# Causal attention in one written-out order of steps, with mask and row minimum in one VectorE instruction, ahead of two feed-forward layers

## The chip, the cores and the metric

The kernel runs on one core of one Trainium2 chip. The metric is the device time of one execution in microseconds (us). A core has five engines that run beside each other, each through its own queue of instructions in order: TensorE (PE in the profile; its weight loads are listed as PEld), VectorE (DVE), ScalarE (ACT), GpSimd (POOL) and SyncE (SP, which here starts the transfers). Matmul results go to PSUM, of which the kernel makes eight banks of 128 x 512 fp32 numbers; everything else lies in SBUF.

## The reference

```python
scores = scale * np.matmul(q, k.transpose(0, 1, 3, 2))      # batch 2, heads 12, seq 448, head_dim 64
scores = np.where(np.triu(ones, k=1), -1e9, scores)
scores = scores - scores.max(-1, keepdims=True)
attn = np.exp(scores)
attn = attn / (attn.sum(-1, keepdims=True) + 1e-09)
x = np.matmul(attn, v)                                       # then (2*448, 12*64) = (896, 768)
h = x @ w_in                                                 # first layer, d_ff 2048
x = (h - np.tanh(h)) @ w_out
y = ((x @ w_a) * (x @ w_b)) @ moe2_w_out                     # second layer, d_ff 1536
```

The weights come in as 64-bit numbers, and the kernel turns them into fp32 itself.

## The kernel before

Attention goes by 12 pairs of heads (2 batches, 6 pairs each; the two heads of a pair are called e = 0 and 1). A pair has four chunks c of 112 query rows; chunk c needs only the first (c+1)*112 keys. So the work is 48 units j = (pair i, chunk c), and a loop over j issues, for every unit, steps of several units at once (a pipeline written by hand).

- `scores(j)` (L254 to L266): q and k of the pair are each split in a high and a low part in fp32r (`qkh`, `qkl`; by `split_qk`, on GpSimd at L248 and L251, for pair 0 on ScalarE at L250), and three products of 64-row operands are summed for each head in a bank of tag `s`. A fourth matmul for each head, of an identity and `mask` in bf16 (L266), adds the causal mask.
- `top(j)`: VectorE takes each head's row maximum from the bank (L271) and scales both by -scale (L272). `exps(j)`: ScalarE reads the bank and writes `p = exp(scale*s + m)` and the row sums (L283). The bank is free only after that.
- `turn_p(j-2)`: TensorE transposes the 112 x 112 blocks of p into banks of tag `t` (L298), which ScalarE (L309) or VectorE (L307) copies to `pt`.
- `values`: twice for each pair, v against `pt`, into the one bank of tag `o` (L319), half h = 0 (chunks 0 and 1) and half h = 1 (chunks 2 and 3).
- `weigh`, `turn_r`: reciprocal of the row sums (VectorE L328, L329), widened on GpSimd (L331), transposed (L337), copied to `y` (ScalarE L346); then x = o * y on VectorE (L349), its high part on ScalarE (L350), its low part on GpSimd (L351). L349 frees bank `o`.

Beside attention two other kinds of work are spread over the loop by the function `filler`. One is the weights' conversion, for each tile of 128 x 768 (or 640): two transfers (L116), a magnitude on ScalarE (L125), four bit operations on VectorE (L142, L144, L148, L152, one at the end of each unit from j = 16 on), a high part on ScalarE (L166) and a low part on GpSimd, after attention on VectorE (L168). The other is the first five hidden chunks of the first layer for batch 0 (`hidden`, 18 matmuls of 448 columns each at L194, all into the one bank of tag `h`): from j = 28 on up to five of these matmuls stand in each unit. When a group of 18 is done, tanh (ScalarE L429) and a subtraction (VectorE L426) must have read the bank before the next group may begin.

The banks are `s` 4, `o` 1, `t` 2, `h` 1. Attention stands in the order of the program text, on every engine. All that comes behind it (the rest of both layers, nearly all matmuls) is ordered by a scheduler at build time, which may also put such work between attention's last steps.

Of the kernel before, what the change touches and what calls it, by code (L numbers as in the profile page):

```python
# [28 lines left out]


# [18 lines left out]
def attention_moe_moe2(ctx, tc, q, k, v, w_in, w_out, w_a, w_b, w_o, out):  # L49
# [5 lines left out]
    XLAG = 7  # L55
    WEIGHTS_AT = 16
    GROUP_P = (2, 4, 3, 4)
# [23 lines left out]
    ident16 = const.tile([128, 128], BF16, name="ident16")  # L81
    mask = const.tile([128, 512], BF16, name="mask")
# [21 lines left out]
    at = {"load": 0, "abs": 0, "bits": 0, "step": 0, "halve": 0, "use": 0, "done": 0}  # L104
# [54 lines left out]
    def split():  # L159
        i = at["halve"]  # L160
        if i >= at["bits"] or i >= at["done"] + len(w_r.turns):
            return
        t = ts.pop(i)
        nk = t.shape[1]
        hi, lo = w_r.tile([([128, KD, 128], F32R, "wh"), ([128, KD, 128], F32R, "wl")])
        nc.scalar.copy(out=hi[:, 0:nk], in_=t.bitcast(F32))  # L166
# [4 lines left out]
        halves[i] = (hi, lo)  # L171
        at["halve"] += 1

# [29 lines left out]
    later_act, later_dve = [], []  # L203
# [3 lines left out]
    def attention(filler):  # L207
        with ExitStack() as st:
            inp = st.enter_context(tc.tile_pool(name="inp", bufs=3))
            pp = st.enter_context(tc.tile_pool(name="p", bufs=1))  # L210
            fixed = st.enter_context(tc.tile_pool(name="fixed", bufs=1))
            sp = st.enter_context(tc.tile_pool(name="small", bufs=4))
# [3 lines left out]
            pts = [fixed.tile([QC, 2, 2 * (h + 1), 2, QC], F32, name=f"pt{h}") for h in range(NQ // 2)]  # L216
            qk, qk2 = {}, {}
            sc, pr, sums, xf, ot = {}, {}, {}, {}, {}
            pairs = [(b, p) for b in range(B) for p in range(NPAIR)]
            units = [(i, c) for i in range(len(pairs)) for c in range(NQ)]  # L220
            def load(i, names):
                if i >= len(pairs):
                    return
                b, p = pairs[i]
                for nm in names:
                    if nm == "v":
                        for e in range(2):
                            nc.sync.dma_start(
                                out=vs[i % NV][:, :, e, :],
                                in_=v[b, 2 * p + e].rearrange("(c s) d -> s c d", s=QC),  # L230
                            )
                    else:
                        if nm == "q":
                            qk[i] = inp.tile([128, 2, S], F32, tag="qk", name="qk")
                        nc.sync.dma_start(
                            out=qk[i][:, int(nm == "k")], in_={"q": q, "k": k}[nm][b, 2 * p:2 * p + 2].rearrange("h d s -> (h d) s")
                        )

            def split_qk(i):

                if i >= len(pairs):
                    return
                hi = inp.tile([128, 2, S], F32R, tag="qkh", name="qkh", bufs=2)
                lo = inp.tile([128, 2, S], F32R, tag="qkl", name="qkl", bufs=2)
                t = qk.pop(i)
                for x in range(2):
                    if i:
                        nc.gpsimd.tensor_copy(out=hi[:, x], in_=t[:, x])  # L248
                    else:
                        nc.scalar.copy(out=hi[:, x], in_=t[:, x])  # L250
                    nc.gpsimd.tensor_tensor(out=lo[:, x], in0=t[:, x], in1=hi[:, x].bitcast(F32), op=ALU.subtract)  # L251
                qk2[i] = hi, lo

            def scores(j):  # L254

                i, c = units[j]
                n = (c + 1) * QC
                cs = slice(c * QC, n)
                sc[j] = [bank("s")[:QC, :n], bank("s")[:QC, :n]]
                hi, lo = qk2[i]  # L260
                for x, (a, b_) in enumerate(((hi, hi), (hi, lo), (lo, hi))):
                    for e in range(2):
                        r = slice(64 * e, 64 * e + 64)
                        nc.tensor.matmul(sc[j][e], a[r, 0, cs], b_[r, 1, :n], start=x == 0, stop=False)  # L264
# [3 lines left out]
            def top(j):  # L268
                m = sp.tile([QC, 2], F32, tag="m", name="m")
                for e, s in enumerate(sc[j]):  # L270
                    nc.vector.tensor_reduce(out=m[:, e:e + 1], in_=s, axis=mybir.AxisListType.X, op=ALU.max)  # L271
                nc.vector.tensor_scalar_mul(out=m, in0=m, scalar1=-scale)  # L272
                pr[j] = m

            def exps(j):
                i, c = units[j]
                n = (c + 1) * QC
                m = pr.pop(j)
                p = pp.tile([QC, 2, n], F32, tag=f"p{c}", name="p")
                if c == 0:  # L280
                    sums[i] = sp.tile([QC, NQ, 2], F32, tag="sum", name="sum", bufs=3)
# [5 lines left out]
                pr[j] = p  # L287

            def turn_p(j):

                i, c = units[j]
                p = pr.pop(j).rearrange("q h (k s) -> q (h k) s", s=QC)
                nb = 2 * (c + 1)
                for a in range(0, nb, GROUP_P[c]):
                    g = GROUP_P[c]
                    pst = bank("t")
                    for x in range(g):
                        nc.tensor.transpose(  # L298
                            out=pst[:QC, x * QC:(x + 1) * QC], in_=p[:, a + x], identity=ident[:QC, :QC]
                        )  # L300
                    out_ = pts[c // 2][:, :, :c + 1, c % 2]
                    if g == nb:
                        in_ = pst[:QC, :g * QC].rearrange("s (e k q) -> s e k q", e=2, q=QC)
                    else:
                        out_, in_ = out_[:, a // g], pst[:QC, :g * QC].rearrange("s (k q) -> s k q", q=QC)
                    if c == 0 or (c >= 2 and a):
                        later_dve.append(lambda o=out_, p=in_: nc.vector.tensor_copy(out=o, in_=p))  # L307
                    else:
                        later_act.append(lambda o=out_, p=in_: nc.scalar.copy(out=o, in_=p))  # L309

            def values(i, h):

                vt, o = vs[i % NV], bank("o") if h == 0 else ot[i]
                ot[i] = o
                for k_ in range(2 * h + 2):
                    c0 = max(2 * h, k_)
                    cs = slice(c0 * QC, (2 * h + 2) * QC)
                    for e in range(2):
                        nc.tensor.matmul(  # L319
                            o[64 * e:64 * e + 64, cs], vt[:, k_, e, :],  # L320
                            pts[h][:, e, k_, c0 - 2 * h:].rearrange("s c q -> s (c q)"),
                            start=k_ == 0, stop=k_ == 2 * h + 1, skip_group_check=True,
                        )

            def weigh(i):

                r = sums.pop(i)
                nc.vector.tensor_scalar_add(out=r, in0=r, scalar1=1e-9)  # L328
                nc.vector.reciprocal(out=r, in_=r)  # L329
                wide = sp.tile([QC, NQ, 2, D], F32, tag="wide", name="wide", bufs=2)  # L330
                nc.gpsimd.tensor_copy(out=wide, in_=r.unsqueeze(3).to_broadcast([QC, NQ, 2, D]))  # L331
                sums[i] = wide

            def turn_r(i):
                r, pst, o = sums.pop(i), bank("t"), ot.pop(i)
                for c in range(NQ):
# [3 lines left out]
                    )  # L340
                b, kk = pairs[i]
                if kk not in xh:
                    xh[kk], xl[kk] = [xp.tile([128, NT], F32R, tag=x, name=x) for x in ("xh", "xl")]
                hi, lo = [t[kk][:, b * S:(b + 1) * S] for t in (xh, xl)]
                x, y = [sp.tile([128, S], F32, tag=t, name=t, bufs=2) for t in "xy"]
                later_act.append(lambda: nc.scalar.copy(out=y, in_=pst[:, :S]))  # L346

                def divide():
                    nc.vector.tensor_tensor(out=x, in0=o[:, :S], in1=y, op=ALU.mult)  # L349
                    nc.scalar.copy(out=hi, in_=x)  # L350
                    nc.gpsimd.tensor_tensor(out=lo, in0=x, in1=hi.bitcast(F32), op=ALU.subtract)  # L351
# [266 lines left out]
```

## Time and profile before

| | us |
|---|---|
| median of 3 runs | 642.12 |
| the runs | 639.67, 642.12, 643.72 |
| span of the profiled execution | 639.7 |
| TensorE busy | 619.0 (97%) |
| VectorE busy | 419.3 (66%) |
| ScalarE busy | 268.2 (42%) |
| GpSimd busy | 82.1 (13%) |

The span of the profiled execution is also its own time; it is as long as the fastest of the three runs, 2.4 us below their median. Busy time counts an instruction from its start to its end, and neighbours on an engine overlap at their ends, so the pitch from one start to the next is somewhat shorter than the duration. [...]

### The profile page before, as it was taken

What the parts mean: (1) busy time and instruction counts of PE and PEld (TensorE: products, weight loads), DVE (VectorE), ACT (ScalarE), POOL (GpSimd) and SP (SyncE); (2) the same over time, 40 slices, a digit from 0 to 9 for tenths busy, and PEclk for the clock granted to TensorE, in tenths of its full rate; (3) what the DMA queues carried; (4) which work ended last, traced back from release to release, by engine and by line L of the source; (5) the groups of instructions that cost most, each with busy time, mean ns of one, the idle gap of its engine ahead of it and who ended that gap; (6) DMA issues with size and microseconds to landing.
All of it is one profiled execution on the core that took longest, in us unless ns stands there. A gap on an engine that the chain in (4) does not pass through costs nothing.

```text
span 639.7 us, 9131 instructions
## 1 busy us (share of the span) xinstructions
PE 619.0 (97%) x3496; PEld 538.7 (84%) x3496; DVE 419.3 (66%) x722; ACT 268.2 (42%) x545; POOL 82.1 (13%) x85
## 2 busy tenths in 40 slices
PE   8999888889999999999999999999999999999997
PEld 4766665567899988998889889999999989999997
DVE  4778655655488899977788986666730489862211
ACT  4777545545265555422544433334421444432000
POOL 4567844422100000000000000000000000000000
PEclk9997778989999999999999999999999999999999
DMA  6443332211144534543333244433230064500111
GB/s 182 120 129 95 94 93 86 56 42 42 42 140 150 189 107 148 172 140 119 112 100 99 99 149 125 123 99 99 99 99 1 2 196 148 162 38 1 50 63 61
DMA packets 64972, 65.08 MB, mean 102 GB/s; under 512 B 13984, under 2 KB 61856, under 8 KB 64928
## 3 DMA queue, kind: packets, MB, share of 16 engines
q1 hardware_dynamic: 64928, 64.50, 32.0%
q8 instruction: 27, 0.44, 0.3%
q14 instruction: 17, 0.14, 0.1%
HBM read 61.73 MB, written 2.75 MB: 101 GB/s over the span
## 4 chain that ended last, share of the span: by engine, by line
PE 92%; DVE 4%; ACT 3%; issue 1%; POOL 0%; ACTq 0%; POOLq 0%; DVEq 0%
PE s L194 39%; PE t L194 18%; PE h L194 13%; PE o L194 9%; PE o L319 4%; PE s L264 4%; PE t L298 3%; ACT p L283 1%; DVE m L271 1%; PE s L266 1%; PE h L479 1%; DVE x L349 1%; ACT pt L309 1%; DVE e L426 0%; ACT y L346 0%
## 5 line engine op out<-in xcount | busy, mean ns | idle before, releaser
L125 ACT ACTIVATE t<-raw 128x768 f32<-128x768 f32 (+1 forms) x70 | 62.0, 885 | 87.0 <-DMA raw<-in_moe_w_out 32.6
L168 DVE TENSOR_TENSOR wl<-t,wh 128x768 fp32r<-128x768 f32 (+1 forms) x62 | 57.7, 934 | 51.8 <-ACT wh L166 51.5
L194 PE MATMUL s<-xh,wl 128*128 128x512 f32 (+2 forms) x222 | 82.8, 373 | 0.0
L194 PE MATMUL s<-xl,wh 128*128 128x512 f32 (+2 forms) x222 | 82.7, 373 | 0.0
L194 PE MATMUL s<-xh,wh 128*128 128x512 f32 (+2 forms) x222 | 82.4, 371 | 0.0
L166 ACT CAST wh<-t 128x768 fp32r<-128x768 f32 (+1 forms) x70 | 56.9, 816 | 44.1 <-PE t L194 12.0
L142 DVE TENSOR_SCALAR t<-t 128x768 f32<-128x768 f32 (+1 forms) x70 | 39.5, 564 | 47.8 <-ACT t L125 47.6
L148 DVE SCALAR_TENSOR_TENSOR t<-raw,t 128x768 int32<-128x768 int32 (+1 forms) x70 | 67.1, 958 | 0.8
L152 DVE SCALAR_TENSOR_TENSOR t<-raw,t 128x768 int32<-128x768 int32 (+1 forms) x70 | 65.0, 929 | 0.9
L283 ACT ACTIVATE p<-s,m 112x112 f32<-112x112 f32 (+3 forms) x96 | 46.7, 495 | 27.1 <-DVE m L272 26.1
L271 DVE TENSOR_REDUCE m<-s 112x1 f32<-112x112 f32 (+3 forms) x96 | 38.5, 442 | 16.0 <-PE s L266 15.3
L414 ACT CAST gwh<-e 128x512 fp32r<-128x512 f32 (+2 forms) x51 | 28.8, 565 | 45.0 <-DVE e L566 37.3
L194 PEld LDWEIGHTS s<-xh,wh 128*128 128x128 f32 x222 | 41.8, 188 | 5.6
L194 PEld LDWEIGHTS s<-xh,wl 128*128 128x128 f32 x222 | 41.7, 188 | 5.6
L194 PEld LDWEIGHTS s<-xl,wh 128*128 128x128 f32 x222 | 41.7, 188 | 5.5
L194 PE MATMUL h<-xh,wh 128*128 128x448 f32 (+2 forms) x84 | 33.8, 402 | 10.8 <-DVE e L426 10.8
L194 PE MATMUL t<-xh,wh 128*128 128x384 f32 (+2 forms) x114 | 40.4, 355 | 0.0
L194 PE MATMUL t<-xh,wl 128*128 128x384 f32 (+2 forms) x114 | 40.4, 354 | 0.0
L194 PE MATMUL t<-xl,wh 128*128 128x384 f32 (+2 forms) x114 | 40.3, 354 | 0.0
L144 DVE TENSOR_SCALAR t<-t 128x768 int32<-128x768 int32 (+1 forms) x70 | 38.0, 543 | 1.0
L298 PE MATMUL t<-ident,p 112*112 112x112 f32 x240 | 36.2, 289 | 0.0
L319 PE MATMUL o<-pt,v 112*64 112x224 f32 (+1 forms) x288 | 33.4, 367 | 2.7 <-DVE x L349 2.4
(140 smaller groups left out, 1369.9 us busy)
## 6 DMA issues: line engine op xcount, KB each, us to landing
raw<-in_moe_w_out SPq DMA_DIRECT2D x48, 384.0 KB, 3.4
raw<-in_moe_w_in SPq DMA_DIRECT2D x32, 384.0 KB, 3.9
raw<-in_moe_w_a SPq DMA_DIRECT2D x24, 384.0 KB, 3.9
raw<-in_moe_w_b SPq DMA_DIRECT2D x24, 384.0 KB, 3.7
raw<-in_moe_w_out SPq DMA_DIRECT2D x12, 256.0 KB, 3.6
qk<-in_q SPq DMA_DIRECT2D x12, 224.0 KB, 4.1
qk<-in_k SPq DMA_DIRECT2D x12, 224.0 KB, 4.2
v<-in_v SPq DMA_DIRECT2D x24, 112.0 KB, 2.5
```

Of the source, the lines that this page charges most:

```text
L125: nc.scalar.activation(out=t.bitcast(F32), in_=raw[:, 0:nk, :, 1].bitcast(F32), func=ACTF.Abs)
L142: nc.vector.tensor_scalar(out=tf, in0=tf, scalar1=LOWEST, scalar2=HIGHEST, op0=ALU.max, op1=ALU.min)
L144: nc.vector.tensor_scalar(out=t, in0=t, scalar1=3, scalar2=0x3FFFFFF8, op0=ALU.logical_shift_left, op1=ALU.bitwise_and)
L148: nc.vector.scalar_tensor_tensor(out=t, in0=low, scalar=29, in1=t, op0=ALU.logical_shift_right, op1=ALU.bitwise_or)
L152: nc.vector.scalar_tensor_tensor(out=t, in0=high, scalar=-0x40000000, in1=t, op0=ALU.bitwise_and, op1=ALU.bitwise_or)
L166: nc.scalar.copy(out=hi[:, 0:nk], in_=t.bitcast(F32))
L168: engine.tensor_tensor(out=lo[:, 0:nk], in0=t.bitcast(F32), in1=hi[:, 0:nk].bitcast(F32), op=ALU.subtract)
L194: nc.tensor.matmul(o, a, b_, start=j == 0, stop=j == n - 1)
L271: nc.vector.tensor_reduce(out=m[:, e:e + 1], in_=s, axis=mybir.AxisListType.X, op=ALU.max)
L283: nc.scalar.activation(out=p[:, e, :], in_=s, func=ACTF.Exp, bias=m[:, e:e + 1], scale=scale, accum_out=sums[i][:, c, e:e + 1],)
L298: nc.tensor.transpose(out=pst[:QC, x * QC:(x + 1) * QC], in_=p[:, a + x], identity=ident[:QC, :QC])
L319: nc.tensor.matmul(o[64 * e:64 * e + 64, cs], vt[:, k_, e, :], pts[h][:, e, k_, c0 - 2 * h:].rearrange("s c q -> s (c q)"), start=k_ == 0, ...
```

## The change

Attention no longer runs in a loop over units. A string `ORDER` names 585 steps, one after the other, and the program is issued in that order; `S3.4` means scores of chunk 3 of pair 4, `S01` chunks 0 and 1 in one pair of banks, `L` mask and minimum, `X` exp, `Tce` and `Cce` transposes and copy of chunk c (0 stands for 0 and 1), head e, `V0` and `V1` the two halves of the values, `A`, `I`, `W`, `R`, `K`, `D`, `H`, `J` the steps from row sums to x, `Q0` to `Q3` the split of q and k, and single letters the spare work: `f` two matmuls of a hidden chunk, `g` one step behind it, `w`, `m`, `b`, `h`, `l` transfers, magnitude, one bit operation, high and low part of a weight tile. It holds 45 `f`, 28 `b`, and 7 each of `m`, `h` and `l`.

What a step does changes too. The mask matmuls are gone. `lows` adds a fp32 mask to the scores on their way from PSUM to `p` in SBUF, negates and scales them and takes the row's minimum in one VectorE instruction (the program shows a second, small one behind it, which writes the minimum out). `exps` then works in place on `p`. Pair 0 isn't split: its scores are one fp32 product. A transpose group may use bank `h` for the first pairs. The add of 1e-9 moves from VectorE to GpSimd; ten warm-up matmuls take the place of sixteen.

```diff
+ORDER = """
+v.2 w S3.0 S01.0 L3.0 L0.0 S2.0 X3.0 L1.0 q.3 L2.0 X0.0 T31.0 X1.0 T30.0 C31.0 C30.0 T00.0 X2.0 T01.0 Q0.2 q.4
...
+L3.2 A.1 C30.1 V0.1 Q1.3 I.1 T20.1 L0.2 X3.2 T21.1 L1.2 k.5 S2.2 W.1 C20.1 C21.1 T31.2 X1.2 L2.2 Q2.3 T30.2 V1.1
...
-    ident16 = const.tile([128, 128], BF16, name="ident16")
-    mask = const.tile([128, 512], BF16, name="mask")
+    warm = const.tile([128, 512], BF16, name="warm")
+    mask = const.tile([128, S], F32, name="mask")
...
+            def split_qk(i, step):
+
+                if i == 0:
+                    qk2[i] = qk[i], None
+                    return
...
+            def scores(i, cs_):
+
+                out = [bank("s"), bank("s")]
+                at_ = 0
+                hi, lo = qk2[i]
+                terms = ((hi, hi),) if lo is None else ((hi, hi), (hi, lo), (lo, hi))
...
-                for e in range(2):
-                    nc.tensor.matmul(sc[j][e][:, cs], ident16[:QC, :QC], mask[:QC, :QC], start=False, stop=True)
...
-                    nc.vector.tensor_reduce(out=m[:, e:e + 1], in_=s, axis=mybir.AxisListType.X, op=ALU.max)
-                nc.vector.tensor_scalar_mul(out=m, in0=m, scalar1=-scale)
...
+                for e, s in enumerate(sc.pop((i, c))):
+                    nc.vector.tensor_tensor_reduce(
+                        out=p[:, e], in0=s, in1=mask[:QC, S - n:], scale=-scale, scalar=3.0e38,
+                        op0=ALU.add, op1=ALU.min, accum_out=least[i][:, c, e:e + 1],
+                    )
...
-                for e, s in enumerate(sc.pop(j)):
                     nc.scalar.activation(
-                        out=p[:, e, :], in_=s, func=ACTF.Exp, bias=m[:, e:e + 1], scale=scale,
+                        out=p[:, e], in_=p[:, e], func=ACTF.Exp, bias=least[i][:, c, e:e + 1], scale=-1.0,
                         accum_out=sums[i][:, c, e:e + 1],
                     )
...
+                pst = bank(("t", "t", "h")[turning[0] % 3] if i + 1 < TURN_WITH_H else "t")
...
+            def add_tiny(i):
+                nc.gpsimd.tensor_scalar_add(out=sums[i], in0=sums[i], scalar1=1e-9)
...
+            for step in ORDER.split():
+                name, _, i = step.partition(".")
+                if i:
+                    run(name, int(i))
+                else:
+                    spare[name]()
...
+    def fill():
+
+        if not fills:
+            f = len(held)
+            held.append(next_weights())
+            new_g(f)
+            fills.append(hidden(held[f], slice(0, S), gh[f, 0], gl[f, 0], bank("h")[:, :S], rests.append, rests.append))
+            fills.append(0)
+        for _ in range(2):
+            next(fills[0])
...
-    keep_warm(8)
-    attention(filler)
+    attention()
```

Two places show how the order changes. The first is TensorE where one group of hidden matmuls ends and the next begins; before, in pair 8 (`h<-` rows are the hidden chunk, `s<-` the scores, `t<-` transposes, `o<-` values):

```order
L194 MATMUL h<-xh,wl 128x448
L264 MATMUL s<-qkh 112x112 x2
L264 MATMUL s<-qkl,qkh 112x112 x2
L264 MATMUL s<-qkh,qkl 112x112 x2
L266 LDWEIGHTS ident_80
L266 MATMUL s<-mask,ident_80 112x112
L266 LDWEIGHTS ident_80
L266 MATMUL s<-mask,ident_80 112x112
L194 MATMUL h<-xh,wh 128x448
L194 MATMUL h<-xl,wh 128x448
```

And the same boundary after the change, with what an instruction waits for in brackets:

```order
L235 MATMUL h<-xl,wh 128x448
L235 MATMUL h<-xh,wl 128x448
L345 MATMUL t<-ident,p 112x112 [waits Activation_49]
L345 MATMUL t<-ident,p 112x112 x2
L371 MATMUL o<-pt_107,v_105 64x224 [waits DMAHW4_49]
L371 MATMUL o<-pt_107,v_105 64x224 [waits DMAHW5_49]
L371 MATMUL o<-pt_107,v_105 64x224 x4
L371 MATMUL o<-pt_107,v_105 64x112 x2
L371 MATMUL o<-pt_106,v_105 64x224 x2
L371 MATMUL o<-pt_106,v_105 64x112 x2
L310 MATMUL s<-qkh 112x336 [waits DVE_49] x2
```

Before, only the scores of a 112-key chunk stand between the two groups; after, transposes, both halves of a pair's values and the scores of two chunks (the second of them, and then the next group's first matmul, follow behind these rows).

The second place is VectorE's queue where weight tiles are converted; before, between pairs 5 and 6 (L142 and L144 are bit operations on a weight tile, L271 and L272 the row maxima, L349 x = o * y, L307 a copy of transposed p):

```order
L142 TENSOR_SCALAR t<-t 128x768
L271 TENSOR_REDUCE m<-s 112x1 x2
L272 TENSOR_SCALAR m<-m 112x2
L349 TENSOR_TENSOR x<-o,y 128x448
L144 TENSOR_SCALAR t<-t 128x768
L271 TENSOR_REDUCE m<-s 112x1 x2
L272 TENSOR_SCALAR m<-m 112x2
L328 TENSOR_SCALAR sum<-sum 112x8
L329 RECIPROCAL sum<-sum 112x8
L307 COPY pt_116<-t 112x3x112
```

And after the change, at the scores of pair 7 (`ISA p,m<-s,mask` is the fused instruction, `ISA m` its small second one):

```order
L178 SCALAR_TENSOR_TENSOR t<-raw,t 128x768
L322 ISA p,m<-s,mask 112x448
L322 ISA m 112x1
L322 ISA p,m<-s,mask 112x448
L322 ISA m 112x1
L380 RECIPROCAL sum<-sum 112x8
L322 ISA p,m<-s,mask 112x112
L322 ISA m 112x1
L322 ISA p,m<-s,mask 112x112
L322 ISA m 112x1
L355 COPY pt_107<-t 112x4x112
L403 TENSOR_TENSOR x<-o,y 128x448
```

Before, a bit operation stands in every unit, ahead of the next unit's row maxima; after, 9 of the 28 stand ahead of the scores of pair 9, and 19 behind them. Each row maximum becomes two instructions, and the scaling is gone.

## Rows read from the trace of the kernel before

**Rows 1.** The page's granted TensorE clock, 40 slices of 16 us, in tenths.

```profile
PEclk9997778989999999999999999999999999999999
```

**Rows 2.** Busy time by stage: us, PE, PEld, DVE, ACT, POOL, clock, DMA share, GB/s.

```profile
0.00:155.25 155.25, 138.07 (x1024) 97.59 (x1025) 100.60 (x249) 89.34 (x268) 77.32 (x81) 0.88 0.33 97
155.25:639.70 484.45, 480.92 (x2473) 441.14 (x2471) 318.67 (x474) 178.91 (x278) 4.75 (x5) 1.00 0.32 103
```

**Rows 3.** The same view in stretches of 10 us.

```profile
30.00:40.00 10.00, 9.66 (x98) 7.09 (x99) 7.98 (x25) 8.23 (x27) 4.98 (x6) 1.00 0.52 154
50.00:60.00 10.00, 9.80 (x66) 6.89 (x68) 8.01 (x16) 6.40 (x20) 8.98 (x7) 0.66 0.25 65
180.00:190.00 10.00, 10.00 (x51) 9.28 (x50) 9.35 (x16) 7.84 (x15) 0.00 (x0) 1.00 0.46 151
```

**Rows 4.** Chain of waits over one pair: start us, us, engine, tile, line, instructions.

```profile
22.70 0.79 PE o L319 x8
23.49 0.49 PE s L264 x6
23.98 0.24 PE s L266 x2
24.22 0.92 PE t L298 x8
25.14 0.65 PE s L264 x6
...
26.22 1.48 PE o L319 x16
27.70 0.79 PE s L264 x6
...
30.21 0.63 DVE x L349
...
30.89 0.79 PE o L319 x8
```

**Rows 5.** Chain of waits behind attention's main part: a run of hidden matmuls.

```profile
155.42 3.85 PE s L194 x19
```

**Rows 6.** TensorE's timeline where a mask matmul stands ahead of a hidden one.

```profile
146.90 0.31 PE L266 MATMUL s<-mask,ident 112*112 112x112 bf16 x2
147.02 0.45 PE L194 MATMUL h<-xh,wl 128*128 128x448 f32 x1
```

**Rows 7.** TensorE's timeline at the end of a hidden group: idle and its releaser in brackets.

```profile
107.53 0.47 PE L194 MATMUL h<-xh,wh 128*128 128x448 f32 x1 [2.75 <-DVE e L426]
108.06 1.24 PE L298 MATMUL t<-ident,p 112*112 112x112 f32 x6
```

**Rows 8.** Who waited for whom, TensorE up to 155.25 us: total, times, longest.

```profile
PE h L194 <- DVE e L426: 10.8, 4, 2.7
PE o L319 <- DVE x L349: 2.4, 4, 1.0
```

**Rows 9.** Groups of instructions on VectorE: busy us, mean ns, idle before them.

```profile
L271 DVE TENSOR_REDUCE m<-s 112x1 f32<-112x112 f32 (+3 forms) x96 | 38.5, 442 | 16.0 <-PE s L266 15.3
L271 DVE TENSOR_REDUCE m<-s 112x1 f32<-112x448 f32 x24 | 13.8, 618 | 5.9 <-PE s L266 5.9
L272 DVE TENSOR_SCALAR m<-m 112x2 f32<-112x2 f32 x47 | 12.9, 274 | 1.6
L349 DVE TENSOR_TENSOR x<-o,y 128x448 f32<-128x448 f32 x10 | 6.2, 623 | 1.8 <-ACT y L346 1.5
```

**Rows 10.** The same up to 155.25 us on ScalarE: a copy from SBUF, one from PSUM.

```profile
L350 ACT CAST xh<-x 128x448 fp32r<-128x448 f32 x10 | 5.6, 563 | 0.0
L346 ACT COPY y<-t 128x448 f32<-128x448 f32 x10 | 5.4, 537 | 0.0
```

**Rows 11.** Chain of waits at the start: warm-up matmuls, then the first scores.

```profile
1.68 3.61 PE h L479 x8
...
7.41 0.43 PE s L264 x6
```

More of the change, by code (lines that the diff above doesn't have):

```diff
@@ L157, in bits_step, with split_high, split_low @@
         at["step"] = (step + 1) % 4
-    def split():
+    def split_high():
+        i = at["high"]
+        if i >= at["bits"] or i >= at["done"] + len(w_r.turns):
+            return
+        nk = ts[i].shape[1]
+        halves[i] = w_r.tile([([128, KD, 128], F32R, "wh"), ([128, KD, 128], F32R, "wl")])
+        nc.scalar.copy(out=halves[i][0][:, 0:nk], in_=ts[i].bitcast(F32))
+        at["high"] += 1
+    def split_low():
         i = at["halve"]
-        if i >= at["bits"] or i >= at["done"] + len(w_r.turns):
+        if i >= at["high"]:
             return
@@ L164, in split @@
         nk = t.shape[1]
-        hi, lo = w_r.tile([([128, KD, 128], F32R, "wh"), ([128, KD, 128], F32R, "wl")])
-        nc.scalar.copy(out=hi[:, 0:nk], in_=t.bitcast(F32))
+        hi, lo = halves[i]
         engine = nc.gpsimd if in_attention else nc.vector
@@ L239, in split_qk @@
[L239 to L252, printed above, removed]
@@ L268, in top @@
[L268 to L282 removed]
+                            r = slice(64 * e, 64 * e + 64)
@@ L283, in exps @@
+            def exps(i, c):
+                p = pr[i, c]
+                for e in range(2):
                     nc.scalar.activation(
-                        out=p[:, e, :], in_=s, func=ACTF.Exp, bias=m[:, e:e + 1], scale=scale,
+                        out=p[:, e], in_=p[:, e], func=ACTF.Exp, bias=least[i][:, c, e:e + 1], scale=-1.0,
                         accum_out=sums[i][:, c, e:e + 1],
                     )
[L287 to L309, printed above, removed]
@@ L314, in values @@
-                ot[i] = o
+                vt = vs[i % NV]
+                if i not in ot:
+                    ot[i] = bank("o")
+                o = ot[i]
                 for k_ in range(2 * h + 2):
@@ L343, in turn_r, with low_x @@
                     xh[kk], xl[kk] = [xp.tile([128, NT], F32R, tag=x, name=x) for x in ("xh", "xl")]
+                nc.scalar.copy(out=xh[kk][:, b * S:(b + 1) * S], in_=xs[i])
+            def low_x(i):
+                b, kk = pairs[i]
                 hi, lo = [t[kk][:, b * S:(b + 1) * S] for t in (xh, xl)]
[L345 to L351, printed above, removed]
@@ L391, in attention @@
-            run(later_act)
-            run(later_dve)
+                engine = nc.vector if i in (5,) else nc.gpsimd
+                engine.tensor_tensor(out=lo, in0=xs.pop(i), in1=hi.bitcast(F32), op=ALU.subtract)
+            steps = {
+                "S01": lambda i: scores(i, (0, 1)), "S2": lambda i: scores(i, (2,)), "S3": lambda i: scores(i, (3,)),
+                "A": add_tiny, "I": invert, "W": widen, "R": turn_r, "K": keep_r, "V0": lambda i: values(i, 0),
+                "V1": lambda i: values(i, 1), "D": divide, "H": high_x, "J": low_x,
+            }
@@ new lines, in attention, with run @@
+            done = set()
+            def run(name, i):
+                if 0 <= i < np_ and (name, i) not in done:
+                    done.add((name, i))
+                    steps[name](i)
+            for i, nm in ((0, "q"), (0, "k"), (1, "q"), (1, "k"), (0, "v"), (2, "q"), (2, "k"), (1, "v")):
+                run(nm, i)
+            keep_warm(WARM)
+            for i in range(2):
+                for c in range(4):
+                    run(f"Q{c}", i)
+            for step in ORDER.split():
+                name, _, i = step.partition(".")
+                if i:
+                    run(name, int(i))
+                else:
+                    spare[name]()
```

268 lines of the change are left out of this document (143 added, 125 removed).

## The prediction

> **What bounds the kernel now.** I read the granted clock first. It falls to 0.7 and 0.8 in slices 4 to 9, from 48 to 144 us, and is 0.9 or more in all others [rows 1]. Cut at 155.25 us, where the fifth hidden group of `filler` is issued, the stage behind has 480.9 us of TensorE work in 484.5 us at clock 1.00, and the stage ahead 138.1 us in 155.25 us at clock 0.88 [rows 2]. Behind the cut TensorE runs pitch to pitch: 19 matmuls of 448 columns in 3.85 us, 0.20 us each [rows 5]. Nothing in attention can shorten that, so the question is where this cut comes to lie. In the stage ahead no engine is full: VectorE is busy 100.6 us, ScalarE 89.3, GpSimd 77.3 [rows 2].
>
> Next the chain of waits over one early pair. Its period, from one set of half-0 values to the next, is 30.89 - 22.70 = 8.19 us [rows 4], in a stretch with clock 1.00 and TensorE busy 9.66 of 10 us [rows 3]. What TensorE does in a pair I add up from the same rows: scores 0.43 (chunk 0, [rows 11]) + 0.49 + 0.65 + 0.79 = 2.36; four mask pairs at 0.24 = 0.96; twenty transposes at 0.92/8 = 0.115, 2.3; four transposes of the reciprocals, taken at the same price, 0.46; values 0.79 + 1.48 = 2.27. The sum is 8.35 us, so at the start attention is bound by TensorE; the VectorE step x = o * y that the chain passes through lasts as long as TensorE work beside it.
>
> Then weights and hidden groups join in and it falls apart. TensorE waited 10.8 us, in four pieces of up to 2.7 us, for VectorE's subtraction (L426) that frees the one bank `h`, and 2.4 us for bank `o` [rows 8]. The piece at 107.5 us shows what follows: 2.75 us idle, and behind it six transposes take 1.24 us where eight took 0.92 before [rows 7, 4]; in 50 to 60 us the clock is 0.66 [rows 3].
>
> **The account of the stage ahead.** First scores start at 7.41 [rows 11]. From there to 155.25 are 147.8 us. TensorE's work in it: 11.6 pairs (the last transposes and values stand behind the cut) at 8.3 less a little for the masks of the later units, which cost 0.12 and not 0.24 where a hidden matmul follows (147.02 - 146.90, [rows 6]): some 94; and 90 hidden matmuls at 0.20, 18. Together 112. So 36 us are lost: the clock takes (1 - 0.88) x 155.25 = 18.6 [rows 2], the two waits 13.2, small things 4.
>
> **The change, part by part.**
> *Mask products.* 48 units lose two small matmuls. About 28 units at 0.24 and 20 at 0.12 [rows 4, 6] make 9.1 us of TensorE work, all in the stage that TensorE limits; between 5.8 (all at 0.12) and 11.5. Work falls to 103.
> *Start.* Warm-up matmuls go from 16 to 10 at 3.61/8 = 0.45 us [rows 11], and pair 0 needs no split. Scores can start at 1.2 + 10 x 0.45 = 5.7 in place of 7.4, 1.7 us earlier; zero if the data lands later. Pair 0's fp32 scores are no row of this trace: I take them as equal to three fp32r products, between 2 us less and 2 us more.
> *Fused mask and minimum.* 96 row maxima take 38.5 us of VectorE, 618 ns at 448 columns; x = o * y, which also reads PSUM and SBUF and writes SBUF, takes 623 ns for 448 [rows 9]. So I put the main instruction at the old price. Its second instruction isn't in the trace: between 0 and the 274 ns of the tiny scaling (L272, [rows 9]); I take the middle, 0.14 x 96 = 13 us. The 47 scalings in this stage go, 12.9 us [rows 9]. VectorE stays at 100.6 - 12.9 + 13 = 101 us. It reached 9.35 of 10 us in the stage behind [rows 3], so it allows a stage of 101/0.935 = 108 us, and hides there unless the stage gets that short.
> [...]
> *Exp in place.* ScalarE now reads SBUF. The nearest rows are a 448-column copy from SBUF at 563 ns and one from PSUM at 537 [rows 10], 26 ns more for each of 96, 2.5 us on an engine with 89 of 155 busy: no cost on the path, and at most 2.5 us if it were. In return a score bank is free after VectorE and not after ScalarE.
> [...]
> *Order.* The hidden groups: the boundary that cost up to 2.7 us now has transposes, a pair's values (2.27 us) and two score units (1.3 us) in it, 3.8 us against the 0.55 to 0.6 us each of tanh and subtraction. I let 2 of the 10.8 us stay. Bit operations (about 0.5 to 1 us each on VectorE) stand mostly behind the scores of pair 9, where hidden matmuls can fill TensorE; ahead of that pair there are 9 in place of some 20. The wait for bank `o` stays, 2 to 3 us, since there is still one. The clock fell after idle stretches and held at 1.00 while TensorE was 97% busy [rows 3, 7]; with most long waits gone I let a third of the 18.6 stay, 6 us. Small waits of four queues that now depend on each other at every step: 9 in place of 4. Loss: 2 + 3 + 6 + 9 = 20 us; bounds are 5 (as in the early pairs) and the old 36.
> *GpSimd and transfers.* Eleven adds of 112 x 8 move there and two splits go; at 77 us it has room. The same 7 weight tiles are converted by the cut as now (7 high and low parts), and transfers take 0.33 of the queues [rows 2]; the stage behind starts with the same stock, so I cost it at nothing. If the stock were short, each missing tile would hold TensorE for some 4 us.
>
> **Sum.** The cut comes to lie at 5.7 + 103 + 20 = 128.7 us in place of 155.25: 26.5 us earlier. The profiled execution took 639.7, the changed one would take 613. The median of the runs lies 2.4 us above the profiled one, so I say 615.5 us for the median; from loss 12 to 28, and mask and start at their bounds, this case holds 603 to 628.
>
> **Rivals.**
> *The order nearly fills TensorE.* Loss 5, as in the early pairs [rows 4]: cut at 113.7, which VectorE's 108 still allows; 598 + 2.4 = 600.5. For it: 1.00 of clock as soon as TensorE is dense. Against: VectorE would have to run at 101/113.7 = 89% with every instruction waiting for another engine.
> *Waits are only moved.* Bank `t` is down to two for the last pairs, every transpose group waits for a copy that stands in VectorE's or ScalarE's queue behind bit operations, idle stretches return and with them the half clock. Loss stays 36: cut at 144.7, 629 + 2.4 = 631.5. If the new order adds another 5 us of half clock it is 636 and not to be told from before.
> *The fused instruction is slow, and VectorE becomes the bound.* With its main part twice the old 0.40 us (38.5/96) and 0.27 for the second, VectorE has 100.6 - 12.9 + 38.5 + 26 = 152 us, at 93.5% a stage of 163: 8 us longer than now, 650 for the median. It decides from the point where both together cost 1.0 us in the mean: then VectorE has 100.6 - 12.9 - 38.5 + 96 = 145 us, 155 at 93.5%, and the change is slower than before. Against it: 623 ns for x = o * y. For it: no row of this form.
>
> **How the numbers follow.** Forecast 0.60; nearly filled 0.15; waits moved 0.16 (0.10 of it faster by over 1%, 0.06 within); slow instruction 0.09 (0.03 within 1%, 0.06 slower). One per cent, 6.4 us, is about what a measurement of this kernel (639.67 to 643.72) can tell from no change. So faster 0.85, within 1% 0.09, slower 0.06. The range that leaves out some 0.08 below and 0.12 above is 598 to 633.
>
> **What would show it.** Right: clock near 1.00 up to the cut, the fifth hidden group issued near 129 us, waits of TensorE for `h` under 3 us in total, the fused instruction at 620 ns for 448 columns, and the same 484 us behind the cut. The mask step is wrong if score pairs still take as long from start to start; the fused step, if its 448-column form is over 0.9 us or the second one over 0.3. I'd be wrong in all if TensorE waits for `wl` behind the cut, since then the weights' conversion, not attention, sets the end.

## The result and the profile after

The changed kernel takes 598.76 us in the median (598.10 to 599.94) against 640.89 for the kernel before on the same chip: ratio 0.935, 95% interval 0.930 to 0.941. The forecast was 615.5, the range 598 to 633: the time lies 0.8 us above its lower edge, where the rival "the order nearly fills TensorE" had put it (600.5). The profiled execution has a span of 597.3 us, 42.4 less than before. (A run's time is longer than its span, here 598.96 against 597.3, so the 639.7 of before, a span, is not the run of 639.67.)

The page's slices of the kernel after, 15 us each: the dip of the granted clock in [rows 1] (the share of TensorE's full speed, in tenths) is gone, and TensorE has hardly a slice below 9.

```profile
PE   8999999999999999999999999999999999999997
DVE  4899999667889998668789866666500988851111
PEclk9999999999999999999999999999999999999999
```

Busy time by stretches of the kernel after (us, PE, PEld, DVE, ACT, POOL, clock, DMA share, GB/s). The first row is the last 484.45 us, as long as the stage behind the cut in [rows 2].

```profile
112.85:597.30 484.45, 479.99 (x2465) 439.22 (x2463) 318.71 (x471) 177.39 (x274) 4.44 (x3) 1.00 0.33 105
...
5.63:112.85 107.22, 103.10 (x914) 79.19 (x914) 97.86 (x288) 88.59 (x269) 75.49 (x83) 1.00 0.43 125
...
40.00:60.00 20.00, 19.22 (x194) 14.85 (x194) 19.56 (x63) 18.58 (x60) 17.25 (x22) 1.00 0.50 136
60.00:80.00 20.00, 19.42 (x168) 15.27 (x170) 19.07 (x53) 17.37 (x52) 14.19 (x14) 1.00 0.41 124
80.00:100.00 20.00, 18.52 (x161) 14.21 (x158) 19.79 (x43) 14.03 (x38) 14.09 (x13) 1.00 0.26 79
```

The last 484 us hold the same TensorE work as before (480.0 against 480.9 of [rows 2]), so all of the gain lies ahead. The cut of the prediction, counted in work, has moved from 155.25 to 112.85. Between the first scores and it are 107.2 us with 103.1 of TensorE work; 4.1 us are lost, where 36 were. VectorE is busy 91% of that stretch, and 95 to 99% from 40 to 100 us, where the two early stretches of before have 80% [rows 3].

The prediction's own sign, the fifth hidden group near 129 us, came true and says less than it seems. That group begins at 114.74, and its last matmul starts at 129.3. But the scheduler has put 62 matmuls of the later stages ahead of that (some 12.5 us at 0.20 each), of which the first stands at 103.61; in the kernel before they began only at 155.25:

```profile
103.61 0.36 PE L235 MATMUL s<-xh,wh 128*128 128x448 f32 x1
...
114.74 0.36 PE L235 MATMUL h<-xh,wh 128*128 128x448 f32 x1
```

So the sign was met in an order that the prediction had not foreseen, and only the cut counted in work shows the gain.

TensorE's waits up to 155 us in the kernel after (total, times, longest), the counterpart of [rows 8]. Neither `h <- e` nor `o <- x` is in the list; the longest wait behind the start is 0.7 us.

```profile
PE t L390 <- ACT pt L353: 1.6, 4, 0.7
PE h L520 <- DVE warm L524: 1.2, 1, 1.2
PE t L345 <- DVE pt L355: 0.9, 3, 0.4
PE s L235 <- ACT ypart L569: 0.5, 1, 0.5
```

Groups of the kernel after up to 155 us (xcount | busy us, mean ns | idle before them), on VectorE and ScalarE; the last row but one is the fused instruction's in the whole page, the last one exp in the kernel before. The listing names the fused instruction CUSTOM_DVE_ANT_0; L172, L178 and L182 are the bit operations that were L142, L148 and L152.

```profile
L322 DVE CUSTOM_DVE_ANT_0 p<-s,mask 112x448 f32<-112x448 f32 x24 | 13.8, 612 | 5.3 <-PE s L310 5.3
L178 DVE SCALAR_TENSOR_TENSOR t<-raw,t 128x768 int32<-128x768 int32 x8 | 10.1, 1264 | 0.1
...
L172 DVE TENSOR_SCALAR t<-t 128x768 f32<-128x768 f32 x8 | 9.0, 1123 | 2.6 <-ACT t L155 2.6
...
L322 DVE DVE_READ_ACCUMULATOR2_ANT m<- 112x1 f32 x96 | 7.8, 82 | 0.0
...
L331 ACT ACTIVATE p<-p,m 112x448 f32<-112x448 f32 x24 | 15.9, 665 | 6.1 <-DVE m L322 6.1
...
L322 DVE CUSTOM_DVE_ANT_0 p<-s,mask 112x448 f32<-112x448 f32 (+3 forms) x96 | 37.6, 440 | 6.3 <-PE s L310 6.2
...
L283 ACT ACTIVATE p<-s,m 112x448 f32<-112x448 f32 x24 | 15.0, 633 | 3.2 <-DVE m L272 3.2
```

The fused instruction costs what the row maximum did (612 against 618 ns at 448 columns, [rows 9]), its read-out 82 ns. The 96 of them keep VectorE busy 37.6 + 7.8 = 45.4 us; maxima and scalings were 38.5 + 12.9 = 51.4 [rows 9]. Exp from SBUF takes 665 ns, from PSUM it took 633 in the profile of before.

TensorE's timeline at the start of the kernel after, beside [rows 11]: ten warm-up matmuls, and scores at 5.63.

```profile
1.25 4.45 PE L520 MATMUL h<-warm 128*128 128x512 bf16 x10 [1.25 <-DVE warm L524]
5.63 1.55 PE L310 MATMUL s<-qk 64*112 64x448 f32 x10
```

**Account of the 42.4 us.** The clock took (1 - 0.971) x 639.7 = 18.6. Now it takes 0.4, all of it at the very end (0.94 over the last 7.3 us, 1.00 before): 18.2. TensorE idles 597.3 - 587.5 = 9.8 us of the span in place of 639.7 - 619.0 = 20.7: 10.9. The remaining 13.3 are TensorE work that is gone: 1.3 of warm-up (sixteen matmuls took 5.73, ten take 4.45), 0.9 behind the cut, and so some 11 ahead of it, most of it the mask products. The account goes by means: idle time at the low clock counts in both of the first two terms.

### The profile page after: what moved, and what is told of

It is laid out like the page before. It is cut to its first block, busy times and chain, and to the rows that moved or that the text cites. A ratio compares the mean times of both kernels' runs of the same rounds, so it can differ in the third digit from the quotient of the medians.

```text
span 597.3 us, 8895 instructions
## 1 busy us (share of the span) xinstructions
PE 587.5 (98%) x3386; PEld 519.7 (87%) x3386; DVE 417.3 (70%) x760; ACT 267.3 (45%) x543; POOL 80.9 (14%) x93
## 4 chain that ended last, share of the span: by engine, by line
PE 82%; DVE 11%; ACT 4%; DMA 1%; POOL 1%; issue 1%; SPq 0%; ACTq 0%; DVEq 0%
PE s L235 40%; PE t L235 19%; PE h L235 10%; PE o L235 9%; DVE p L322 3%; ACT p L331 2%; DVE pt L355 2%; DVE t L178 1%; DVE t L172 1%; DMA raw<-in_moe_w_out 1%; DVE t L182 1%; PE o L371 1%; PE h L520 1%; DVE x L403 1%; DVE t L174 1%
## 5 line engine op out<-in xcount | busy, mean ns | idle before, releaser
L178 DVE SCALAR_TENSOR_TENSOR t<-raw,t 128x768 int32<-128x768 int32 (+1 forms) x70 | 69.4, 992 | 1.0
L182 DVE SCALAR_TENSOR_TENSOR t<-raw,t 128x768 int32<-128x768 int32 (+1 forms) x70 | 68.6, 980 | 0.8
L172 DVE TENSOR_SCALAR t<-t 128x768 f32<-128x768 f32 (+1 forms) x70 | 43.5, 621 | 34.1 <-ACT t L155 33.8
L331 ACT ACTIVATE p<-p,m 112x448 f32<-112x448 f32 (+3 forms) x96 | 49.7, 523 | 9.1 <-DVE m L322 9.1
L322 DVE CUSTOM_DVE_ANT_0 p<-s,mask 112x448 f32<-112x448 f32 (+3 forms) x96 | 37.6, 440 | 6.3 <-PE s L310 6.2
L235 PE MATMUL h<-xh,wh 128*128 128x448 f32 (+2 forms) x84 | 31.3, 372 | 0.3
L235 PE MATMUL h<-xl,wh 128*128 128x448 f32 (+2 forms) x84 | 31.5, 375 | 0.0
L345 PE MATMUL t<-ident,p 112*112 112x112 f32 x202 | 29.7, 265 | 1.6 <-DVE pt L355 0.9
L235 PE MATMUL h<-xh,wl 128*128 128x448 f32 (+2 forms) x84 | 31.1, 370 | 0.0
```

Source lines behind the costliest of these rows:

```text
L172: nc.vector.tensor_scalar(out=tf, in0=tf, scalar1=LOWEST, scalar2=HIGHEST, op0=ALU.max, op1=ALU.min)
L178: nc.vector.scalar_tensor_tensor(out=t, in0=low, scalar=29, in1=t, op0=ALU.logical_shift_right, op1=ALU.bitwise_or)
L182: nc.vector.scalar_tensor_tensor(out=t, in0=high, scalar=-0x40000000, in1=t, op0=ALU.bitwise_and, op1=ALU.bitwise_or)
L235: nc.tensor.matmul(o, a, b_, start=j == 0, stop=j == n - 1)
L322: nc.vector.tensor_tensor_reduce(out=p[:, e], in0=s, in1=mask[:QC, S - n:], scale=-scale, scalar=3.0e38, op0=ALU.add, op1=ALU.min, accum_o ...
L331: nc.scalar.activation(out=p[:, e], in_=p[:, e], func=ACTF.Exp, bias=least[i][:, c, e:e + 1], scale=-1.0, accum_out=sums[i][:, c, e:e + 1],)
```

## The experiments

The prediction gave the mask products 9.1 us, the order 16 (a loss of 20 in place of 36), the new VectorE and ScalarE instructions nothing (theory A). The rival is that the order is worth so much only because these instructions make room for it (theory B). So I took the change apart from both sides: parts of it put into the kernel before, and parts of it undone in the kernel after. All ratios are against the kernel before.

**From the side of the kernel before.** Four runs keep its loop.

*Only the instructions* (mask and minimum in one, exp in place, no mask products; in the loop of before):

```diff
-                nc.tensor.matmul(sc[j][e][:, cs], ident16[:QC, :QC], mask[:QC, :QC], start=False, stop=True)
...
-                    nc.vector.tensor_reduce(out=m[:, e:e + 1], in_=s, axis=mybir.AxisListType.X, op=ALU.max)
-                nc.vector.tensor_scalar_mul(out=m, in0=m, scalar1=-scale)
+                    nc.vector.tensor_tensor_reduce(
+                        out=p[:, e], in0=s, in1=mask[:QC, S - n:], scale=-scale, scalar=3.0e38,
+                        op0=ALU.add, op1=ALU.min, accum_out=m[:, e:e + 1],
...
```

> The loop of before with the new instructions: no mask products, mask and minimum in one VectorE instruction, exp in place. Theory A (the order brings most: waits for bank h and the half clock go with it, the instructions only take the mask products' 9 us of TensorE away): 628 to 633 us, waits for h still near 11 us, clock still under 0.98. Theory B (the instructions bring most, because a score bank is free before exp and the masks no longer stand on TensorE): 600 to 615, clock near 1.

630.96 us, ratio 0.987 (0.982 to 0.992): inside the 628 to 633 of theory A, far from the 600 to 615 of theory B. TensorE's wait for the subtraction is what it was in [rows 8], in a profile of the fastest of the four runs (625.51):

```profile
PE h L194 <- DVE e L427: 11.7, 4, 2.9
```

*No mask products, nothing else* (the two matmuls of L266 go):

> The kernel before without the mask products, which leaves the causal mask out. If TensorE's time is what counts in that stage, 5.8 to 11.5 us less than before (629 to 635). Rival: they lie beside waits for VectorE and ScalarE, then 0 to 3 us less.

639.42 us, ratio 0.999 (0.995 to 1.003): some 9 us of TensorE work removed, and nothing gained that ten runs could tell. (The kernel leaves the causal mask out; the other instructions stay.) The wait for `h` stays:

```profile
PE h L194 <- DVE e L424: 12.5, 4, 3.4
```

The clock between 40 and 100 us stands at 0.83, where before has 0.83, 0.83 and 0.74 in its three stretches of 20 us. TensorE is busy 611.6 us of this profile, 7.4 less than before, and idle 24.8 in place of 20.7: more than half of the work that was taken away came back as waiting.

*A longer rest between hidden groups* in the kernel before, its only edit:

```diff
-                rest_until[0] = j + 1
+                rest_until[0] = j + 2
```

> The kernel before with one unit more between two hidden groups. If the 10.8 us wait for bank h and a part of the half clock that follows it are a real loss, the wait falls under 3 us and the time by 8 to 18 us (622 to 633). Rival: TensorE then waits for the next step in its queue instead, and the time falls by 0 to 4 us.

625.93 us, ratio 0.980 (0.975 to 0.985). The wait for `h` all but goes:

```profile
PE h L194 <- DVE e L426: 1.3, 2, 0.8
```

This one number is worth no less than all instructions of the change in the old loop; the two intervals overlap.

*Instructions and longer rest together:*

> The loop of before with the new instructions and one unit more between two hidden groups. If the two parts only add up (9 and 14 us alone): 615 to 619. If the early release and the gap help each other as instructions and order do: under 612, with the wait for bank h under 3 us and the clock at 0.99.

613.37 us, ratio 0.957 (0.951 to 0.964), so 4.3% where the two alone add up to 3.3%. The time lies between the two expectations, and the intervals are about as wide as that difference: that the two help each other is likely and not settled. The old loop with two edits reaches two thirds of the gain; the written-out order is not needed for that part.

**From the side of the kernel after.**

*Only the order* (mask products, maximum and scaling, and exp from PSUM as before, in the new order):

```diff
-                    nc.vector.tensor_tensor_reduce(
...
+                    nc.vector.tensor_reduce(
+                        out=least[i][:, c, e:e + 1], in_=s, axis=mybir.AxisListType.X, op=ALU.max
                     )
+                nc.vector.tensor_scalar_mul(out=least[i][:, c], in0=least[i][:, c], scalar1=-scale)
...
```

> The new order with the old instructions: mask products on TensorE, row maximum and scaling on VectorE, exp from PSUM. A: 605 to 613 (the changed kernel's 599 plus 6 to 12 for mask products and scalings), clock 0.99 or more. B: 625 to 640, score banks held until exp stop TensorE again, clock under 0.98.

633.08 us, ratio 0.989 (0.986 to 0.992): outside the 605 to 613 of theory A, inside the 625 to 640 of theory B. The order by itself (with the shorter start, the unsplit pair 0 and the third transpose bank) is worth as little as the instructions by themselves. Its clock of 0.981 takes 12.0 us, against 0.4 in the kernel after. In its trace TensorE waits for score banks that are free only after ScalarE:

```profile
PE s L311 <- ACT p L333: 8.9, 13, 2.4
```

and among VectorE's groups the scaling of 112 x 2 numbers, 274 ns in [rows 9], takes 510 in the mean:

```profile
L327 DVE TENSOR_SCALAR m<-m 112x2 f32<-112x2 f32 x48 | 24.5, 510 | 1.7
```

The next three each undo one of the pieces in the kernel after.

*Mask products back on TensorE* (beside the fused instruction):

```diff
...
+                    for e in range(2):
+                        nc.tensor.matmul(sc[i, c][e][:, cs], ident16[:QC, :QC], mask16[:QC, :QC], start=False, stop=True)
```

> The changed kernel with the 96 mask products of before put back on TensorE (the mask is then added twice, which changes nothing in the result); all else stays new. Theory C (the new order pays because a score bank is free after VectorE; the mask products are small beside that): 600 to 611 us, in it 6 to 12 more than the changed kernel if TensorE binds there, 0 to 4 if VectorE does. Theory D (the order pays only without mask products on TensorE): 620 or more.

608.67 us, ratio 0.950 (0.945 to 0.956), 9.9 us over the kernel after, as theory C has it. With clock 1.00 this is the price of the work itself, 48 pairs at 0.21 us. In the old loop the same matmuls were worth nothing.

*Score banks released late* (exp reads the scores again, so that a bank is free only after ScalarE):

```diff
...
-                        out=p[:, e], in_=p[:, e], func=ACTF.Exp, bias=least[i][:, c, e:e + 1], scale=-1.0,
+                        out=p[:, e], in_=s, func=ACTF.Exp, bias=least[i][:, c, e:e + 1], scale=scale,
```

> The changed kernel, but exp reads the scores from PSUM again, so that a score bank is held until ScalarE is done; the exponent then leaves the causal mask out (the minimum still has it). Instruction counts stay those of the changed kernel. C: 618 to 635, TensorE waits some 9 us for exp as with the order alone, and the clock falls. D: 597 to 605.

608.71 us, ratio 0.951 (0.945 to 0.956), 10.0 us over the kernel after. (The exponent leaves the causal mask out here.) Both expectations missed: the time lies between the 618 to 635 of theory C and the 597 to 605 of theory D, so the early release is worth 10.0 us here, and not all that the kernel with only the order lacks. TensorE waits as it did with the order only:

```profile
PE s L310 <- ACT p L331: 6.2, 13, 1.8
```

*One small VectorE instruction more for each unit,* of the shape of the scaling that the change removed:

```diff
+                nc.vector.tensor_scalar_mul(out=least[i][:, c], in0=least[i][:, c], scalar1=1.0)
```

> The changed kernel with one more small VectorE instruction in each of the 48 units, a product of the minimum with 1.0, some 0.17 to 0.27 us each. If VectorE now binds attention: 8 to 13 us slower (607 to 612). If TensorE does: 0 to 3 us.

621.53 us, ratio 0.970 (0.964 to 0.976), 22.8 us over the kernel after, where I expected 8 to 13 at the most. Its group on VectorE:

```profile
L326 DVE TENSOR_SCALAR m<-m 112x2 f32<-112x2 f32 x48 | 26.9, 560 | 1.7
```

Little hides it: 26.9 us more of VectorE cost 22.8 of time. The clock takes (1 - 0.989) x 620.0 = 6.8 in this run, against 0.4. Exp needs what this instruction writes, and waits for it (us, times, up to 60 us):

```profile
  ACT p L332: 14.7, 9
```

Whether the 22.8 come from a full VectorE or from the longer way from minimum to exp is not told apart by this run. The same line's summary up to 60 us (shortest, median and longest, ns) says that the long ones are long by something outside them:

```profile
L326 DVE TENSOR_SCALAR m<-m x24: 169/446/1193, 8.3 to 56.5; 112x2 f32<-112x2 f32 x24
```

What that is shows in the timelines of this run, first VectorE (start, us):

```profile
42.84 0.53 DVE L326 TENSOR_SCALAR m<-m 112x2 f32<-112x2 f32 x1
...
44.49 1.19 DVE L326 TENSOR_SCALAR m<-m 112x2 f32<-112x2 f32 x1
...
46.57 0.84 DVE L326 TENSOR_SCALAR m<-m 112x2 f32<-112x2 f32 x1
```

and GpSimd in the same stretch:

```profile
42.79 0.56 POOL L290 CAST qkh<-qk 128x448 fp32r<-128x448 f32 x1
...
44.53 1.14 POOL L292 TENSOR_TENSOR qkl<-qk,qkh 128x448 fp32r<-128x448 f32 x1
...
46.24 1.14 POOL L292 TENSOR_TENSOR qkl<-qk,qkh 128x448 fp32r<-128x448 f32 x1
```

Each of the three ends with the GpSimd instruction beside it: 43.37 and 43.35, 45.68 and 45.67, 47.41 and 47.38. All six between 42 and 54 us took over 0.2 us, 0.29 to 1.19, and ended 0.01 to 0.03 us behind a GpSimd instruction. That GpSimd is what holds them is my reading of this, which the next two kernels test. (The fused instruction, from PSUM and SBUF to SBUF, shows no such stretch: at 448 columns it takes 612 ns in the kernel after and 617 in the kernel without the split that follows.)

*The same instruction without the split of q and k.* If GpSimd is what stretches it, it must get cheaper when most of GpSimd's work goes. Two kernels, the first without the extra instruction:

```diff
-                if i == 0:
+                if True:
                     qk2[i] = qk[i], None
```

> The changed kernel with q and k of all pairs left unsplit, as pair 0's already are: 44 GpSimd instructions (41 us) go, and the scores are fp32 products, which cost TensorE some 0.35 us more for each of 11 pairs (1.74 us for chunks 3, 0 and 1 of pair 0 against 1.4 of pair 1), 4 us. Theory E (GpSimd's SBUF instructions stretch VectorE's bit operations from about 0.95 to 1.45 us, and VectorE binds): VectorE's bit operations fall under 1.1 us in the mean, 590 to 598 us. Rival (TensorE binds as well, and its 4 us count in full): 601 to 606.

> The unsplit kernel with the extra small VectorE product in each unit. Theory E: without GpSimd's split beside it this instruction takes 0.2 to 0.3 us and not 0.56, and it costs 8 to 14 us over the unsplit kernel, not 22. Rival (its cost is the dependence between minimum and exp, whatever GpSimd does): 20 to 25 us over it, and its duration stays above 0.45 us.

With it 623.13 us (ratio 0.971, 0.965 to 0.978), without it 611.16 (0.953, 0.946 to 0.960): 12.0 us for the extra instruction in place of 22.8, inside the 8 to 14 expected. Its mean is 366 ns in place of 560, above the 0.2 to 0.3 us expected; up to 60 us its median is that of an undisturbed one:

```profile
L326 DVE TENSOR_SCALAR m<-m x30: 169/170/2162, 8.7 to 59.9; 112x2 f32<-112x2 f32 x30
```

The longest took 2.16 us; what held it is not shown. The median, 170 ns where it was 446, came out as contention with GpSimd has it.

But the kernel without the split is itself 12.4 us slower than the kernel after, outside both of its expectations (590 to 598 and 601 to 606). Its trace has a chain of long waits between 40 and 100 us that accounts for most of it: ScalarE waits for a weight tile, VectorE for ScalarE, and TensorE for a subtraction that stands behind that in VectorE's queue.

```profile
DVE t L172 <- ACT t L155: 13.0, 1, 13.0
ACT t L155 <- DMA raw<-in_moe_w_in: 12.7, 1, 12.7
...
PE h L235 <- DVE e L483: 11.4, 1, 11.4
```

The run with the extra instruction has the same wait (11.3 us at the longest). So the 12.0 us are the instruction's price in a kernel that also stands still for 11 us, and are the weaker half of this test; in a kernel without that wait the instruction was not tried.

The waits of SyncE's transfer queue (L273 issues q and k, L146 weights) name a cause, transfers of q and k that stand until the scores have read an earlier pair's buffer, with the weights' transfers behind them in the same queue:

```profile
SPq L146 <- DVE t L182: 61.4, 10, 11.6
SPq L273 <- PE s L310: 49.4, 8, 15.3
```

The first row is no sign by itself: it is 66.6 us in the kernel after. The second is, since there q and k wait for the split and not for the scores, 16.9 us in all. Without a split, q and k keep their three buffers until the scores are done.

*Five buffers in place of three* for the unsplit q and k put that to the test:

```diff
-                    qk[i] = inp.tile([128, 2, S], F32, tag="qk", name="qk")
+                    qk[i] = inp.tile([128, 2, S], F32, tag="qk", name="qk", bufs=5)
```

> The kernel after with queries and keys of all pairs left unsplit, as in the run without the split, and in addition 5 buffers instead of 3 for the unsplit queries and keys. The run without the split lost 12.4 us against the kernel after (611.16 against 598.76); 11.4 us of it stand as one wait of TensorE in the weight stage (h <- DVE e) and its clock fell to 0.74 behind that. In its trace the transfer of a later pair's queries waited 15.3 us on SyncE for the scores that still read the buffer, and the weight transfers stand behind it in that queue. Theory Q (the queue is the whole loss): no transfer of queries waits over 5 us, no wait of TensorE for e over 3 us, clock 1.00 in the first 150 us, time 592 to 600 us, as the kernel after or a little faster. Theory F (the unsplit scores themselves cost the loss, or VectorE without the split's company has another limit): the wait of SyncE for queries goes, but the time stays at 604 to 612 us.

595.86 us in the median (595.26 to 596.52, six runs), ratio 0.931 (0.927 to 0.935), as theory Q has it: the queue was the cause. Its wait on the scores is down to this row:

```profile
SPq L273 <- PE s L310: 1.6, 1, 1.6
```

and of TensorE's waits no one behind the start is over 0.5 us. All six times lie below the kernel after's lowest, by 2.9 us between the medians; the two were not timed together, and the intervals of the two ratios overlap (0.930 to 0.941 and 0.927 to 0.935), so that it is faster than the kernel after is likely and not settled. VectorE's groups in this run show where it has more room:

```profile
L178 DVE SCALAR_TENSOR_TENSOR t<-raw,t 128x768 int32<-128x768 int32 x9 | 10.0, 1106 | 0.1
...
L172 DVE TENSOR_SCALAR t<-t 128x768 f32<-128x768 f32 x9 | 6.3, 705 | 1.9 <-ACT t L155 1.9
```

705 ns where the kernel after has 1123, and 1106 where it has 1264.

*One copy of each pair moved from VectorE to ScalarE* in the kernel after:

```diff
-    ACT_KEEPS = {(0, 0), (2, 0), (3, 0)}
+    ACT_KEEPS = {(0, 0), (2, 0), (3, 0), (0, 1)}
```

> The changed kernel with one more of the six copies of a pair on ScalarE (chunk 0, head 1), 12 copies of 0.50 us less on VectorE and 12 of 0.44 more on ScalarE. If VectorE alone binds: 3 to 6 us less (593 to 596). If ScalarE is as full: no change, or 2 to 6 us more.

600.53 us, ratio 0.936 (0.931 to 0.942): no gain, as expected if ScalarE is as full as VectorE.

```profile
20.00:40.00 20.00, 18.99 (x188) 14.05 (x184) 17.73 (x59) 18.47 (x63) 16.95 (x21) 1.00 0.51 145
40.00:60.00 20.00, 18.81 (x191) 14.99 (x191) 17.64 (x60) 18.70 (x63) 15.54 (x22) 1.00 0.48 129
```

VectorE falls to between 17.4 and 17.9 of every 20 us between 20 and 100 us, so it isn't the only limit. ScalarE stays at 18.5 and 18.7 of 20 in these two stretches (18.4 and 18.6 in the kernel after): with more to do it is no busier. That ScalarE is what binds there is argued; TensorE is as busy.

## Why the prediction was right in kind and wrong in size

**The step that failed is "Loss: 2 + 3 + 6 + 9 = 20 us".** By the prediction's own formula it measured 4.1 (112.85 - 5.63 - 103.1). That is 16 us too much, and nearly all of the 16.7 by which the forecast missed. That the range still holds the time, by 0.8 us, is owed to its width; the rival with a loss of 5 had both the time and the reason, the clock at 1.00 where TensorE is dense (busy 18.5 to 19.4 of every 20 us from 20 to 100 us). The other terms held: work of 103 us came out as 103.1, the start at 5.7 as 5.63, the stage behind at 484 with the same work.

- *Wait for `h`*, 2 left: 0 measured. *Wait for `o`*, 3 left: none in the list.
- *Clock*, 6 left: nothing, since the 0.4 that it takes lie at the kernel's end. I scaled the old loss by a guess. The rows show it at 1.00 in every stretch of the kernel after up to 590 us, in which no wait of TensorE behind the start is over 0.7 us; in before, with waits of up to 2.7 [rows 8], it fell to 0.66 from 50 to 60 us [rows 3] and to 0.50, the half clock of the prediction, from 90 to 96 us.
- *Small waits*, 9: 4.1. "Every instruction waiting for another engine" was also my argument against the rival, which needs VectorE at 89%. It runs at 95 to 99% from 40 to 100 us.
- *VectorE* "hides, unless the stage gets that short": it did get that short. From 5.63 to the cut VectorE is busy 97.9 of 107.2 us. The read-out took 82 ns and not 140, 7.8 us in place of 13, but longer bit operations took part of that back.
- *Exp in place*, "no cost on the path": right as far as the runs go, 32 ns more at 448 columns than in before, where the copies had said 26. What I credited in half a sentence, the bank free after VectorE, is worth 10.0 us in this order.
- *Mask products, 9.1*: 9.9 in the new order, 0 in the old. *Fused instruction at the old price*: 612 ns forecast as 618 to 623; the rival of a slow one fell with that, since its main part at twice the old price is in no run, and the rival of waits only moved with the clock.
- A reading: of the six slices that I put at 0.7 and 0.8, one, from 112 to 128 us, stands at 0.9 [rows 1]. The sum takes the clock from [rows 2] and stays.

**What the sum had no place for** is that the parts don't add. It gave the order 16 us and the mask products 9.1 as if each came by itself; by themselves they brought 6.6 (633.08 against 639.71) and 0.3 (639.42). In the old loop or alone they gave 1.3% (instructions) and 1.1% (order), together 6.5%. Undone one at a time from the other end they cost 9.9 (mask), 10.0 (bank) and 22.8 (a small instruction on VectorE), 42.7 in sum, against 34.3 for all three in the kernel with only the order. In the old loop removed work turned into waiting at the hidden groups and elsewhere (for `h` 12.5 us without the mask products, 10.8 in before; TensorE idle 24.8 and 20.7); once those waits are gone, from 20 us on TensorE and VectorE are nearly full up to 100 and ScalarE up to 60, and each of the three pieces counted at about its full price. That fullness is the reason is argued: taking 12 copies off VectorE gained nothing. I costed the scaling at 12.9 us of an engine with room, which hides it; in the new order such instructions take 24.5 to 26.9 us on an engine without.

**Open.** The run with the extra instruction undoes the scaling by adding an instruction of that shape, not the scaling itself; that the two cost alike is argued from their means, 510 and 560 ns. How the 18.2 us of clock divide among the waits that went was not tried apart from the longer rest, which alone leaves a clock of 0.87 and 0.91 in the first 100 us.

## What to carry to other kernels

Before adding up what the parts of a change save, ask what the stage waits for: here work removed from an engine whose real limit was a wait came back as waiting (9 us of matmuls worth 0), and the same work counted in full once the wait was gone (9.9 us). A stage in which every engine has "room" under one order may have none under a better one (VectorE at 80% in two stretches before, at 95 to 99% after), so cost small instructions by what they would be on a full engine, beside what runs on the others then (169 ns at the least, 560 in the mean). When a step that copied data out of a buffer goes, look at who held that buffer and what stands behind it in the transfer queue (here a wait of up to 15.3 us).

## What the runs showed of the hardware

A VectorE instruction on 112 x 2 numbers in SBUF took 169 ns at the least and 1.19 us beside a GpSimd subtraction, ending with it; in the kernel before, whose 274 ns in the mean [rows 9] I had taken for its price, most took 169. All 14 that took over 0.2 us there ended 0.02 to 0.04 us behind a GpSimd instruction. The bit operations were stretched as well: 1123 ns for L172 in the attention stage of the kernel after, 705 without the split of q and k and with five buffers. In the kernel after the five of L172 that took 1.15 us or more each ended 0.35 to 0.43 us behind a GpSimd instruction; beside an idle GpSimd one took 0.49 to 0.56 us. The instruction that adds a mask from SBUF to scores in PSUM, writes the sum to SBUF and keeps the row's minimum cost no more than a row maximum alone (612 and 618 ns at 448 columns), with a read-out of 82 ns behind it.
